# Sliding the right-side tiles of SBUF by 480 bytes in a gated attention and SwiGLU kernel

## The chip, the cores and the metric

The kernel runs on one core of a Trainium2 chip. The metric is the device time in microseconds of one execution, as a median over runs. The core has five engines with instruction queues of their own: TensorE (PE; its weight loads are shown apart as PEld), VectorE (DVE), ScalarE (ACT), GpSimd (POOL) and SyncE (SP), which here only issues transfers. They work on SBUF, the on-chip memory of 128 partitions, and on PSUM, into which TensorE writes its sums. A tile is an area of SBUF that has the same byte address in every partition.

## The reference

```python
def _A_ref(x, wqkv, wo):                       # x: 1 x 2048 x 512, H = 32 heads of 16
    qkv = (x @ wqkv).reshape(B, S, 3, H, Dh)...
    scores = jnp.einsum("bhqd,bhkd->bhqk", q, k) * Dh ** -0.5
    o = jnp.einsum("bhqk,bhkd->bhqd", softmax(scores), v)
    return o.transpose(0, 2, 1, 3).reshape(B, S, D) @ wo

def _B_ref(x, w1, w3, w2):                     # F = 1792
    return (silu(x @ w1) * (x @ w3)) @ w2

g = sigmoid((x * gate_w).sum(-1, keepdims=True))
out = g * _A_ref(x, wqkv, wo) + (1 - g) * _B_ref(x, w1, w3, w2)
```

All inputs and the output are float32.

## The kernel before

The work is one attention layer with 32 heads over 2048 positions, one SwiGLU layer, and a mix of the two. Products that need float32 accuracy are made of three products of rounded halves (type float32r): high by high, high by low, low by high. A matrix thus appears as two tiles, such as xH and xL for x, fh and fl or wh and wl for weights. In a matmul call the second argument is the stationary operand (the weights that LDWEIGHTS puts into the array), the third the moving one, which streams 512 columns past it.

**Where tiles lie.** SBUF is filled by two stacks. From the left come the pools const, xp (xH0 to xL3, 8 KB each), vp (V), qkp (Qt and Kt, two of each) and, later, wk (p0 to p9 of 4 KB and u of 2 KB). From the right end come fw (slots fr, fh1, fl1, fh3, fl3), fk (slots gw, raw, sg, hx, gs), all of 2048 bytes a partition, and p1 (xn, wh, wl, hi, lo and three small ones), which only the first stage uses. `slot(tag)` takes from fw if the tag begins with f, otherwise from fk. When p1 is closed (`ph1.close()`), wk is opened on the left and grows over the room that p1 had. The names in the profile leave buffer numbers out, so fh stands for fh1 and fh3, and xH also for the tiles that later reuse xp's places (w2H, w2L, Oh, Ol).

**First stage.** x is loaded into xn, transposed by TensorE, and rounded into xH and xL. `project_qk` (L181) multiplies the first 128 columns of Q and of K with weights wh and wl from p1; `project_v`, by `three` (L95 to L97), makes V with xH or xL stationary and the halves fh, fl of the weights moving. `bound` and `guard_rows` work out whether the scores are small enough for a softmax without row maxima; the flag is read at the branch of `row_maxima` (L278, `tc.If`), which all engines pass. Ahead of it SP issues the Q and K transfers for the first heads (L254, L261), and `load_weights(chunks[0])` (L314) loads the first weights, which POOL splits (L321, L322).

**Main stage.** TensorE's order is written out by hand as a string, one letter for each piece of work:

```python
one = "QFFF" * 7 + "QPPPP"
two = ["QFFF" * 5 + "QPPQQPP", "QFFF" * 6 + "PPQQPP"]
order = "QQFFF" + one * LONG + "".join(two[...] for i in range(short))   # LONG = 83, short = 44
```

- Q is `score` (L719): for two heads at once, in the array's rows 0 to 63 and 64 to 127, Kt is stationary (50 rows) and Qt moving, into one of two PSUM tiles S. ScalarE turns S into p by exp (L723).
- F is `feed`: up to two matmuls of 64 rows, "upper" and "lower", each with weights of its own, of a product that has nothing to do with attention. In turn these are `w_product` (L409: the other Q and K columns, then w1 and w3; stationary are the halves in fh, fl, raw or gw, moving xH or xL), `h_product` (L518: the SwiGLU's last product; stationary are tiles of fw and fk that hold h by the list SETS, moving the halves of w2 in xp), and `o_product` (L597: part of the output projection; stationary are again tiles of fw and fk).
- P is `pv` (L706): V is stationary (17 columns), p moving, four at once for two units and two heads, into acc. `evac` (L687) copies acc to u after each head pair.

So a long period holds 8 Q, 21 F and 4 P, a short one 8 Q, 15 F and 4 P. VectorE copies out the sums and works on the silu (L432 to L458), POOL splits later weights (L488, L489) and multiplies by reciprocals (L578).

**Last stage.** Two row blocks of the output projection take their weights (ot) from raw and gw; then eight blocks take them from xp and, for the last quarter, from tiles of wk that VectorE has just written (L816). All use `three`, twelve matmuls of 128 rows a block, with wo in xp and wk tiles moving.

Of the kernel before, what the change touches and what calls it, by code (L numbers as in the profile page):

```python
# [8 lines left out]
F32 = mybir.dt.float32  # L9
# [8 lines left out]
P = 128  # L18
# [15 lines left out]
def gated_mix_kernel(ctx: ExitStack, tc: tile.TileContext, x, wqkv, wo, w1, w3, w2, gate_w, out):  # L34
# [25 lines left out]
    xp = ctx.enter_context(tc.tile_pool(name="xp", bufs=1))  # L60
    vp = ctx.enter_context(tc.tile_pool(name="vp", bufs=1))
    qkp = ctx.enter_context(tc.tile_pool(name="qkp", bufs=1))
    fw = ctx.enter_context(tc.tile_pool(name="fw", bufs=2, side="right"))
    fk = ctx.enter_context(tc.tile_pool(name="fk", bufs=2, side="right"))
    ph1 = ExitStack()
# [782 lines left out]
```

## Time and profile before

| | |
|---|---|
| median of 3 runs | 1423.19 us (1422.14 to 1423.74) |
| span of the profiled execution, first to last instruction | 1417.6 us |
| median less that span | 5.6 us |
| TensorE busy | 1408.8 us, 99% |
| ScalarE busy | 1033.2 us, 73% |
| VectorE busy | 449.4 us, 32% |
| GpSimd busy | 321.1 us, 23% |
| HBM traffic | 98 GB/s over the span |

The profile gives one execution. Its times run from the first instruction on. In a view in order of time, a row gives the start and the length in us, the engine, the line, the operation, output<-inputs with the moving operand ahead of the stationary one, and how many instructions are merged (x2). A busy time of TensorE contains overlap: matmuls are pipelined, and the next begins before the last has drained, so the distance of two starts tells more than the length of one. In a view of groups the numbers behind the bar are the busy time in us and the mean length of one in ns; in a view of one line they are the least, median and greatest length in ns. A window row gives the stretch, its length, then the busy time and count of each engine.

### The profile page before, as it was taken

The numbers are of one execution on the slowest core, as the hardware profiler recorded it, in microseconds if no ns is written. First come the engines' busy times: TensorE is split into PE (matmuls) and PEld (weight loads), VectorE is DVE, ScalarE is ACT, GpSimd is POOL, SyncE is SP. The second block draws the span as 40 slices with busy tenths as digits, with TensorE's granted clock in tenths as the row PEclk, the third lists the DMA queues.
The fourth block names the chain that finished last, engine by engine and source line by source line (L and its number), as shares of the span: only waits on it lengthen the run. The fifth ranks groups of instructions, "written<-read, shape, count | busy, mean of one in ns | idle before, by whom it ended". The sixth has DMA issues, their size and how long they took to land.

```text
span 1417.6 us, 28518 instructions
## 1 busy us (share of the span) xinstructions
PE 1408.8 (99%) x11399; PEld 833.7 (59%) x11399; DVE 449.4 (32%) x845; ACT 1033.2 (73%) x1153; POOL 321.1 (23%) x356
## 2 busy tenths in 40 slices
PE   9999999999999999999999999999999999999998
PEld 7865656656556566565565665655555555554556
DVE  4421102464555545455464545400000000000013
ACT  4556767777777777777777777777788778877870
POOL 5014443011011100110110015441332332233230
PEclk9999999999999999999999999999999999999999
DMA  7554455342124432223233234543534443345445
GB/s 197 141 121 114 126 140 128 73 110 69 46 61 85 113 69 61 70 72 87 68 76 79 76 81 122 136 101 74 126 81 102 104 105 70 66 112 106 106 133 182
DMA packets 112668, 141.42 MB, mean 100 GB/s; under 512 B 16400, under 2 KB 70672, under 8 KB 109456
## 3 DMA queue, kind: packets, MB, share of 16 engines
q1 hardware_dynamic: 110384, 135.72, 39.6%
q10 hardware_dynamic: 2144, 3.80, 0.8%
q8 instruction: 92, 1.51, 0.5%
q14 instruction: 48, 0.39, 0.1%
HBM read 90.70 MB, written 48.76 MB: 98 GB/s over the span
## 4 chain that ended last, share of the span: by engine, by line
PE 93%; POOL 0%; DMA 0%; DVE 0%; ACT 0%; issue 0%; SPq 0%; ACTq 0%; POOLq 0%
PE acc L706 32%; PE f L409 27%; PE S L719 19%; PE f L518 11%; PE f L597 1%; PE f L95 0%; PE f L97 0%; PE f L96 0%; DMA fr<-in_B_w_dram 0%; PE S L97 0%; PE S L96 0%; PE S L95 0%; POOL xL L489 0%; POOL fl L489 0%; DVE sg L458 0%; POOL xH L488 0%
## 5 line engine op out<-in xcount | busy, mean ns | idle before, releaser
L723 ACT ACTIVATE p<-S 128x1024 f32<-128x1024 f32 x1024 | 967.5, 1026 | 308.4 <-PE S L719 307.1
L706 PE MATMUL acc<-p,V 128*17 128x512 f32 x4096 | 473.5, 594 | 0.0
L719 PE MATMUL S<-Qt,Kt 50*128 50x512 f32 x2048 | 427.9, 413 | 1.1 <-POOLq L278 0.6
L719 PEld LDWEIGHTS S<-Qt,Kt 50*128 50x128 f32 x2048 | 193.8, 184 | 187.4 <-ACT p L723 80.4
L706 PEld LDWEIGHTS acc<-p,V 128*17 128x17 f32 x4096 | 102.8, 97 | 274.1 <-issue 273.9
L409 PE MATMUL f<-xL,fh 64*128 64x512 f32 x1024 | 205.1, 391 | 0.0
L409 PE MATMUL f<-xH,fl 64*128 64x512 f32 x1024 | 204.9, 390 | 0.0
L409 PE MATMUL f<-xH,fh 64*128 64x512 f32 x1024 | 204.7, 390 | 0.0
L440 DVE RECIPROCAL sg<-sg 128x64 f32<-128x64 f32 x448 | 201.2, 509 | 1.9
L409 PEld LDWEIGHTS f<-xL,fh 64*128 64x128 f32 x1024 | 99.4, 187 | 21.2
L409 PEld LDWEIGHTS f<-xH,fl 64*128 64x128 f32 x1024 | 98.5, 185 | 20.1
L409 PEld LDWEIGHTS f<-xH,fh 64*128 64x128 f32 x1024 | 99.4, 187 | 17.7
L321 POOL CAST fh<-fr 128x512 fp32r<-128x512 f32 x32 | 21.6, 674 | 371.1 <-DMA fr<-in_B_w_dram 246.5
L687 DVE COPY u<-acc 128x512 f32<-128x512 f32 x32 | 22.1, 692 | 257.0 <-PE acc L706 257.0
L518 PE MATMUL f<-xH,fl 64*128 64x512 f32 x224 | 82.2, 391 | 0.5 <-POOL fl L489 0.5
L518 PE MATMUL f<-xL,fh 64*128 64x512 f32 x224 | 82.2, 391 | 0.3 <-POOL xL L489 0.3
L518 PE MATMUL f<-xH,fh 64*128 64x512 f32 x224 | 82.1, 391 | 0.0
L518 PE MATMUL f<-xH,raw 64*128 64x512 f32 x192 | 74.9, 390 | 0.0
L532 DVE TENSOR_SCALAR gs<-f,omg 128x512 f32<-128x512 f32 x16 | 12.0, 751 | 176.4 <-PE f L518 176.4
L432 DVE COPY gs<-f 128x512 f32<-128x512 f32 x56 | 38.7, 691 | 78.1 <-PE f L409 78.1
L518 PE MATMUL f<-xH,fr 64*128 64x512 f32 x160 | 62.4, 390 | 0.0
L454 DVE TENSOR_TENSOR raw<-f,gs 128x512 f32<-128x512 f32 x50 | 34.1, 682 | 82.7 <-PE f L409 82.7
(216 smaller groups left out, 1309.6 us busy)
## 6 DMA issues: line engine op xcount, KB each, us to landing
Kt<-kH_d SPq DMA_DIRECT2D x128, 128.0 KB
h_d<-sg SPq DMA_DIRECT2D x56, 256.0 KB
sg<-h_d SPq DMA_DIRECT2D x43, 256.0 KB
fr<-in_B_w_dram SPq DMA_DIRECT2D x42, 256.0 KB
Qt<-qH_d SPq DMA_DIRECT2D x128, 64.0 KB
Kt<-kL_d SPq DMA_DIRECT2D x64, 128.0 KB
fr<-in_A_wqkv_dram SPq DMA_DIRECT2D x18, 256.0 KB
Qt<-qL_d SPq DMA_DIRECT2D x64, 64.0 KB
```

The lines of the kernel that those rows point to most:

```text
L321: nc.gpsimd.tensor_copy(wh, r)
L409: nc.tensor.matmul(ps, w[i == 2][r, k, :], (xL if i == 1 else xH)[b][r, k, :], start=n == 0 and r.start == 0, stop=n == 3 * ND - 1 and r.s ...
L432: nc.vector.tensor_copy(gs, ps)
L440: small.append(lambda q=q: nc.vector.reciprocal(sg[:, q:q + 64], sg[:, q:q + 64]))
L454: nc.vector.tensor_mul(gu, ps, st["gs"])
L518: nc.tensor.matmul(ps, hs[t][q][i == 2][r, P * o:P * o + P], (w2L if i == 1 else w2H)[q][r, o, :], start=n == 0 and r.start == 0, stop=n = ...
L532: nc.vector.tensor_scalar(y, ps, omg[:, t:t + 1], None, op0=OP.mult)
L597: nc.tensor.matmul(ps, ot[t][i == 2][r, P * k:P * k + P], wo_[k][i == 1][r, :], start=n == 0 and r.start == 0, stop=n == 3 * ND - 1 and r. ...
L687: nc.vector.tensor_copy(u, acc)
L706: nc.tensor.matmul(acc[r:r + DH + 1, :], V[:, k, 2 * j + h, :], p[:, h, :], start=k == 0, stop=k == NT - 1)
L719: nc.tensor.matmul(ps[:, h, :], Kt[i][r:r + 50, P * k:P * k + P], Qt[i][r:r + 50, t:t + 512], start=True, stop=True)
L723: nc.scalar.activation(p, ps, AF.Exp, scale=SCALE)
```

## The change

A pool with one tile of 480 bytes a partition (120 float32) is opened on the right side ahead of all others. Nothing reads or writes it. It is never closed before the end, so every tile of fw, fk and p1 begins 480 bytes lower: at a multiple of 64 bytes, where it was 32 bytes past one. The left pools and every instruction stay as they are.

```diff
     qkp = ctx.enter_context(tc.tile_pool(name="qkp", bufs=1))
+    top_pad = ctx.enter_context(tc.tile_pool(name="top_pad", bufs=1, side="right"))
+    top_pad.tile([P, 120], F32, name="top_pad")
     fw = ctx.enter_context(tc.tile_pool(name="fw", bufs=2, side="right"))
     fk = ctx.enter_context(tc.tile_pool(name="fk", bufs=2, side="right"))
```

## The prediction

> **What bounds the kernel now.** I read the page first, then the order of time on TensorE in one period of the main stage, then the last thirty microseconds, then the chain of waits at the few places where TensorE stops.
>
> ```profile
> span 1417.6 us, 28518 instructions
> PE 1408.8 (99%) x11399; PEld 833.7 (59%) x11399; DVE 449.4 (32%) x845; ACT 1033.2 (73%) x1153; POOL 321.1 (23%) x356
> PEclk9999999999999999999999999999999999999999
> PE 93%; POOL 0%; DMA 0%; DVE 0%; ACT 0%; issue 0%; SPq 0%; ACTq 0%; POOLq 0%
> ```
>
> TensorE works 99% of the span at full clock, and 93% of the chain that ended last is its own work. So a change counts by what it does to the pitch of matmuls, the time from one start to the next. One period shows that pitch. In a name like f<-xH,fh the first operand is the moving one, the second the stationary one (the weights, loaded ahead by LDWEIGHTS).
>
> ```profile
> 256.10 0.40 PE L719 MATMUL S<-Qt,Kt 50*128 50x512 f32 x2
> 256.33 0.39 PE L409 MATMUL f<-xH,fh 64*128 64x512 f32 x2
> 256.56 0.40 PE L409 MATMUL f<-xL,fh 64*128 64x512 f32 x2
> 256.80 0.40 PE L409 MATMUL f<-xH,fl 64*128 64x512 f32 x2
> 257.03 0.40 PE L719 MATMUL S<-Qt,Kt 50*128 50x512 f32 x2
> ...
> 261.67 0.39 PE L719 MATMUL S<-Qt,Kt 50*128 50x512 f32 x2
> ```
>
> Rows of x2 are two 64-row matmuls that share the array. From 256.10 to 261.67 there are six cycles of one score pair and three feed pairs, 24 starts in 5.57 us: 0.928 us a cycle, 232 ns a pair. Nothing here waits; the question is whether 232 ns is the floor. The end of the kernel answers it. There the output projection runs 128-row matmuls of the same 512 columns, first with weights from right-side tiles (raw, gw), then from left-side tiles (xH, xL, p).
>
> ```profile
> 1386.63 0.40 PE L95 MATMUL f<-xH,raw 128*128 128x512 f32 x1
> ...
> 1391.30 0.39 PE L97 MATMUL f<-p,gw 128*128 128x512 f32 x1
> 1391.53 0.39 PE L95 MATMUL S<-xH,xH 128*128 128x512 f32 x1
> ...
> 1412.61 0.39 PE L95 MATMUL S<-p,p 128*128 128x512 f32 x1
> ```
>
> By the code (twelve matmuls a block of 128 rows) 21 start from 1386.63 up to 1391.53: 233.3 ns each. From there to 1412.61 it is 93: 226.7 ns each. The step falls on the first matmul with left-side weights; the moving tiles are the same (xH, xL, p) on both sides of it, and the pitch then holds to the end, whichever PSUM tile is written. The shape view says it too:
>
> ```profile
> L95 PE MATMUL f<-p,raw 128*128 128x512 f32 x4 | 1.6, 394 | 0.0
> L95 PE MATMUL S<-p,xH 128*128 128x512 f32 x4 | 1.6, 389 | 0.0
> L95 PEld LDWEIGHTS f<-p,raw 128*128 128x128 f32 x4 | 0.8, 188 | 0.2
> L95 PEld LDWEIGHTS S<-p,xH 128*128 128x128 f32 x4 | 0.8, 188 | 0.2
> ```
>
> The same moving p is streamed in 394 ns with right-side weights and in 389 ns with left-side ones, while the load itself reads 188 ns in both. So a tax of 233.3 - 226.7 = 6.6, say **6.7 ns a matmul**, sits on weights from the right side. What differs about these tiles is where they begin: the change says 32 bytes past a multiple of 64, while the layout of the left pools (xp, qkp, wk) puts xH, xL, Kt, Qt and p at multiples of 512. The right side can be taxed as a moving operand as well:
>
> ```profile
> L95 PE MATMUL f<-fh,xH x64: 392/396/502, 23.5 to 83.9; 128*128 128x512 f32 x64
> L95 PE MATMUL S<-xH,xH x8: 389/389/389, 1391.5 to 1398.3; 128*128 128x512 f32 x8
> ```
> In the projection of V, fh moves and xH is the weight: never below 392 ns, median 396, against 389 in all eight of the last stage.
>
> **The change part by part.** No instruction is added or removed; every tile of fw, fk and p1 slides down by 480 bytes. All their slots (2048 bytes in fw and fk) and the weight slices (512 bytes) are multiples of 64, so one slide moves all of them from 32 past to 0. The tiles of wk take over p1's room later; worked out from the sizes, each of p0 to p9 and u lies over the same p1 tiles after the slide as before, so no wait is added.
>
> *Feed matmuls.* Their weights are all right-side tiles (fh, fl, raw, gw, fr, hx).
>
> ```profile
> 0.00:1417.60 1417.60, 472.52 (x3264) 315.40 (x3264) 1.00 0.41 100
> 0.00:1417.60 1417.60, 206.84 (x1344) 137.55 (x1344) 1.00 0.41 100
> 0.00:1417.60 1417.60, 27.50 (x144) 18.33 (x144) 1.00 0.41 100
> ```
>
> These are the matmuls of L409, L518 and L597 over the whole span: 3264 + 1344 + 144 = 4752, in pairs 2376. Is the tax a pair's, too? The steady cycle has three taxed pairs and one score pair with left operands: 4 x 226.7 + 3 x 6.7 = 926.9 ns, where 928 was read. The sum fits the pair as it fits the single matmul, so 2376 x 6.7 = **15.9 us** go, all on the path. Bounds: nothing, if the right side itself is what costs, and 2376 x 7.2 = 17.1 us if the whole cycle's excess over 4 x 226.7 (21 ns, three ways 7.1) goes. I take 6.7, the row that compares tiles directly. The 24 late matmuls of the tail give 24 x 6.7 = 0.2 us.
>
> *Early stage.* 192 matmuls with moving fh or fl and 96 with weights wh, wl (L181) carry about 7 ns each, 2.0 us at most. But what opens the main stage is not TensorE:
>
> ```profile
> 63.22 1.09 PE L181 MATMUL S<-xH,wl 128*128 128x512 f32 x4
> 76.31 2.19 SPq L314 DMA_DIRECT2D fr<-in_A_wqkv_dram  x2
> 81.27 0.61 POOL L321 CAST raw<-fr 128x512 fp32r<-128x512 f32 x1 [43.43 <-DMA fr<-in_A_wqkv_dram]
> 83.90 1.28 POOL L322 TENSOR_TENSOR gw<-fr,raw 128x512 fp32r<-128x512 f32 x1
> 85.33 0.93 PE L719 MATMUL S<-Qt,Kt 50*128 50x512 f32 x4 [0.61 <-POOLq L278]
> ```
>
> The branch at L278 waits for POOL's split of the first weights, which waits for a load issued at 76.31, behind SP's row of Q and K transfers that began with the last L181 product. So only what TensorE saves before 64.3 us arrives: nine of 16 V tiles (108 matmuls) and the 96, less those that ran in the first 26 us beside loads. About 140 x 6.7 = **0.9 us**, between 0 and 2.0.
>
> *V as weights* (L706) and p as its stream stay where they are, on the left; a block of 32 keeps its time.
>
> ```profile
> 251.57 3.56 PE acc L706 x32
> ```
>
> *Other users of the moved tiles* are priced by left and right rows of one shape:
>
> ```profile
> L687 DVE COPY u<-acc 128x512 f32<-128x512 f32 x32 | 22.1, 692 | 257.0 <-PE acc L706 257.0
> L432 DVE COPY gs<-f 128x512 f32<-128x512 f32 x56 | 38.7, 691 | 78.1 <-PE f L409 78.1
> L578 POOL TENSOR_TENSOR p<-p 128x512 f32<-128x512 f32 x6 | 7.7, 1288 | 0.0
> L489 POOL TENSOR_TENSOR fl<-sg,fh 128x512 fp32r<-128x512 f32 x23 | 29.6, 1287 | 1.8
> ```
>
> 692 against 691 and 1288 against 1287 ns: zero. Transfers into the moved tiles could go either way; TensorE's work hides them except at the two places shown here (the load above, 81.27 - 76.31 = 5.0 us, and the one below), and I take zero, with 1 us either way (a tenth of the 5.0 us at each). Without that cover, a load's 5 us would count whole.
>
> *Who is late next.* Two things do not shrink with TensorE.
>
> ```profile
> L723 ACT ACTIVATE p<-S 128x1024 f32<-128x1024 f32 x1024 | 967.5, 1026 | 308.4 <-PE S L719 307.1 <-ACT p L723 1.3
> 255.66 6.61 ACT L723 ACTIVATE p<-S 128x1024 f32<-128x1024 f32 x7 [2.97 <-PE S L719]
> 1118.79 1.94 ACT L723 ACTIVATE p<-S 128x1024 f32<-128x1024 f32 x2 [1.25 <-PE S L719]
> 909.52 0.69 DVE hx L454
> ...
> 922.64 0.50 PE f L518
> ```
>
> Two exps back to back take 1.94 us, and one takes 1.026 (its group's mean), so ScalarE's own pitch is 0.92 us. Today a score comes every 0.928; afterwards every 4 x 226.7 = 0.907, so ScalarE falls behind by 14 ns a score for the seven scores up to the block of L706. The slack is there: the exp that began at 255.66 ended near 256.69, and the score that reuses its PSUM tile began at 257.03, 0.34 us later; after the change at worst 0.34 - 2 x 0.02 - 6 x 0.014 = 0.21 remain. Queued behind a blocked score are the three feed pairs and the L706 block, so it would cost TensorE directly; I take 0.3 us in all for places already tight. The other is a chain of 13.1 us from VectorE (909.52) over a load and POOL to TensorE (922.64); TensorE, 1.3% faster there, waits 0.2 us longer. In the tail the last operand is split in time:
>
> ```profile
> 1404.94 0.69 DVE L816 TENSOR_TENSOR p<-fr,p 128x512 fp32r<-128x512 f32 x1 [0.70 <-ACT p L815]
> ```
> It ends at 1405.6. The last 24 matmuls read it; the one at 1412.61 is the 22nd of them, so the first starts at 1412.61 - 21 x 0.2267 = 1407.85, 2.2 us later, far more than the 0.2 us that the tail gains.
>
> **The sum.** 15.9 + 0.2 + 0.9 - 0.3 - 0.2 = 16.5 us off the profiled 1417.6: a span of 1401.1. The median of the runs, 1423.19, is 5.6 above the span; I keep that: **1406.7 us**.
>
> **The rivals.** *ScalarE takes over.* If the slack does not carry, each run of eight scores is paced at 0.921 instead of 0.907: 7 x 14 = 98 of the 141 ns (21 x 6.7) saved per long period come back, and 5 x 14 = 70 of 100 (15 x 6.7) per short one. With 83 long and 44 short periods by the code, 83 x 43 + 44 x 30 = 4.9 us remain, with the early 0.9 some 5.8: 1417.4. For it: 0.92 is above 0.907. Against: 0.34 us of slack, a fresh start after every L706 block.
>
> *The side, not the residue.* If weights from these tiles are slow because they were just written by POOL, or lie high in SBUF, the slide does nothing: 1423. For it: no row has a right-side tile at a multiple of 64. Against: the moving fh is taxed alike, long after it was written; and the last 24 matmuls take their weights p 2.2 us after VectorE wrote them, at 226.7 ns.
> The Trainium skill (SBUF — State Buffer, Specifications) has SBUF cachelines of 16 bytes and a penalty for each crossing to a new one. By that rule 512 contiguous bytes cross equally often from 32 past as from 0, so the change would be worth nothing and this rival's time would hold; the trace's 394 against 389 disagrees unless the side is the cause.
>
> *A collision, slower.* After the slide the tiles of fw and fk begin at multiples of 512 bytes, at the same residue as the stream xH that runs while they load; today they lie 480 past. If two reads at equal places collide, from the first feed pair on, at a price like today's tax on top of it, 2376 x 6.7 = 15.9 come on: 1439. Against: in the tail both operands are at multiples of 512 and run fastest.
>
> **How the numbers follow.** Forecast 70%, ScalarE 13%, no effect 11%, collision 6%. The forecast's own range is 1403 to 1410 (early and transfers 2 us, the tax's bounds 1 us, waits 3 us). The range for 8 in 10 takes in the ScalarE case: 1402.5 to 1418. Within 0.2%, 2.8 us, is what can't be told from no change: faster 0.83, same 0.11, slower 0.06.
>
> **What would show it.** The cycle from 256.10 should read 0.907 instead of 0.928, matmuls of L95 with raw weights 389 instead of 394, fh as moving operand 389. A block of L706 stays at 3.56 us. If scores begin to wait on L723 in every period, ScalarE has taken over; if raw still reads 394, the residue was not the cause, and the prediction is wrong.

## The result and the profile after

The change brings no gain: a median of 1420.63 us over 14 runs (1419.80 to 1426.29), against 1420.56 us (1417.92 to 1423.74) for 14 runs of the kernel before. The ratio is 1.0006, with a 95% interval of 0.9995 to 1.0018. The forecast was 1406.7 us, its range 1402.5 to 1418. In some executions the granted clock halves for some 9 us early in the main stage, which costs about 5 us (last section); those without it, told by their clock or, for the kernel before, by their time, take 1419.80 to 1421.01 us after the change and 1417.92 to 1418.97 before, so that like for like the change costs about 1.5 us.

From the page of the kernel after: the span, the engines, and the groups of the scores and of the feeds (all line numbers are two higher than before).

```profile
span 1417.7 us, 28518 instructions
PE 1409.3 (99%) x11399; PEld 833.6 (59%) x11399; DVE 448.7 (32%) x845; ACT 1035.4 (73%) x1153; POOL 320.5 (23%) x356
L721 PE MATMUL S<-Qt,Kt 50*128 50x512 f32 x2048 | 426.9, 412 | 1.4 <-POOLq L280 0.9
L411 PE MATMUL f<-xH,fh 64*128 64x512 f32 x1024 | 207.3, 396 | 0.0
L411 PE MATMUL f<-xL,fh 64*128 64x512 f32 x1024 | 205.5, 392 | 0.0
L411 PE MATMUL f<-xH,fl 64*128 64x512 f32 x1024 | 204.5, 390 | 0.0
```

The feeds, which were to become 6.7 ns cheaper, read 396, 392 and 390 ns. Before, the same groups read 390, 391 and 390:

```profile
L409 PE MATMUL f<-xL,fh 64*128 64x512 f32 x1024 | 205.1, 391 | 0.0
L409 PE MATMUL f<-xH,fl 64*128 64x512 f32 x1024 | 204.9, 390 | 0.0
L409 PE MATMUL f<-xH,fh 64*128 64x512 f32 x1024 | 204.7, 390 | 0.0
```

Only the feed that comes right behind a score has changed, and for the worse. The kernel after in order of time on TensorE, at five places:

```profile
83.64 0.93 PE L721 MATMUL S<-Qt,Kt 50*128 50x512 f32 x4 [0.87 <-POOLq L280]
...
253.86 0.50 PE L721 MATMUL S<-Qt,Kt 50*128 50x512 f32 x2
...
255.83 0.40 PE L721 MATMUL S<-Qt,Kt 50*128 50x512 f32 x2
256.06 0.40 PE L411 MATMUL f<-xH,fh 64*128 64x512 f32 x2
256.30 0.40 PE L411 MATMUL f<-xL,fh 64*128 64x512 f32 x2
256.53 0.39 PE L411 MATMUL f<-xH,fl 64*128 64x512 f32 x2
...
260.49 0.39 PE L721 MATMUL S<-Qt,Kt 50*128 50x512 f32 x2
...
264.37 0.50 PE L721 MATMUL S<-Qt,Kt 50*128 50x512 f32 x2
...
1386.06 0.50 PE L97 MATMUL f<-xH,raw 128*128 128x512 f32 x1
1386.39 0.40 PE L98 MATMUL f<-xL,raw 128*128 128x512 f32 x1
...
1388.93 0.39 PE L97 MATMUL f<-xH,raw 128*128 128x512 f32 x1
...
1391.65 0.39 PE L97 MATMUL S<-xH,xH 128*128 128x512 f32 x1
```

- The first score starts at 83.64 instead of 85.33. Other profiles with the same first stage scatter: 84.60, 85.11 and 85.36 without the pad (runs of the experiments below), 83.90 and 84.45 with it. The means, 85.10 and 84.00, are 1.1 us apart.
- Five cycles of one score and three feeds take 260.49 - 255.83 = 4.66 us, 0.932 a cycle, where 0.928 was read before. A long period (first score behind a block of L708 to the next such score) is 264.37 - 253.86 = 10.51 us. Its median over the main stage went from 10.495 to 10.518, that of a short period from 9.427 to 9.433.
- From the first score to the first matmul of the last stage it is now 1386.06 - 83.64 = 1302.4 us; before it was 1385.83 - 85.33 = 1300.5. So the main stage lost 1.9 us and gave the early gain back; the medians of the periods say the same, 83 x 0.023 + 44 x 0.006 = 2.2 us.
- In the last stage, the second block with weights from raw and gw (twelve matmuls, 1388.93 to 1391.65) runs at 226.7 ns, as predicted, where it ran at 233.3. The block ahead of it does not yet: 11 starts from 1386.39 to 1388.93 are 231 ns apart.

So the tail shows the effect, the main stage does not. In V's projection it shows as well, in the first products of Q and K only in part: their medians go from 397 to 393 or 394 ns, not to 389 (rows of two lines of the kernel after, least, median and greatest length in ns):

```profile
L97 PE MATMUL f<-fh,xH x64: 388/389/496, 22.9 to 81.9; 128*128 128x512 f32 x64
L183 PE MATMUL S<-xH,wl x32: 387/394/496, 11.3 to 62.4; 128*128 128x512 f32 x32
```

### The profile page after: what moved, and what is told of

Same layout as the page of the kernel before. It is cut to its first block, busy times and chain, and to the rows that moved or that the text cites. A ratio compares the mean times of both kernels' runs of the same rounds, so it can differ in the third digit from the quotient of the medians.

```text
span 1417.7 us, 28518 instructions
## 1 busy us (share of the span) xinstructions
PE 1409.3 (99%) x11399; PEld 833.6 (59%) x11399; DVE 448.7 (32%) x845; ACT 1035.4 (73%) x1153; POOL 320.5 (23%) x356
## 4 chain that ended last, share of the span: by engine, by line
PE 92%; POOL 1%; DMA 1%; SPq 0%; issue 0%; ACT 0%; DVE 0%; ACTq 0%; POOLq 0%
PE acc L708 32%; PE f L411 27%; PE S L721 19%; PE f L520 11%; PE f L599 1%; DMA fr<-in_B_w_dram 1%; POOL xL L491 0%; PE f L97 0%; PE f L98 0%; PE f L99 0%; SPq L256 0%; PE S L98 0%; PE S L97 0%; PE S L99 0%; POOL xH L490 0%
## 5 line engine op out<-in xcount | busy, mean ns | idle before, releaser
L725 ACT ACTIVATE p<-S 128x1024 f32<-128x1024 f32 x1024 | 969.9, 1027 | 308.0 <-PE S L721 306.7
L708 PE MATMUL acc<-p,V 128*17 128x512 f32 x4096 | 473.5, 594 | 0.0
L721 PE MATMUL S<-Qt,Kt 50*128 50x512 f32 x2048 | 426.9, 412 | 1.4 <-POOLq L280 0.9
L721 PEld LDWEIGHTS S<-Qt,Kt 50*128 50x128 f32 x2048 | 194.4, 184 | 187.9 <-ACT p L725 79.8
L708 PEld LDWEIGHTS acc<-p,V 128*17 128x17 f32 x4096 | 102.7, 97 | 273.4 <-issue 273.2
L411 PE MATMUL f<-xH,fh 64*128 64x512 f32 x1024 | 207.3, 396 | 0.0
L520 PE MATMUL f<-xH,fh 64*128 64x512 f32 x224 | 83.0, 395 | 0.0
```

What stands on the lines that cost most here:

```text
L411: nc.tensor.matmul(ps, w[i == 2][r, k, :], (xL if i == 1 else xH)[b][r, k, :], start=n == 0 and r.start == 0, stop=n == 3 * ND - 1 and r.s ...
L520: nc.tensor.matmul(ps, hs[t][q][i == 2][r, P * o:P * o + P], (w2L if i == 1 else w2H)[q][r, o, :], start=n == 0 and r.start == 0, stop=n = ...
L708: nc.tensor.matmul(acc[r:r + DH + 1, :], V[:, k, 2 * j + h, :], p[:, h, :], start=k == 0, stop=k == NT - 1)
L721: nc.tensor.matmul(ps[:, h, :], Kt[i][r:r + 50, P * k:P * k + P], Qt[i][r:r + 50, t:t + 512], start=True, stop=True)
L725: nc.scalar.activation(p, ps, AF.Exp, scale=SCALE)
```

## The experiments

Each run below is called after its question. Most of these kernels were run once. Their times stand beside a time of the kernel before that was taken with them; the argument rests on pitches, not on these times.

**Three other sizes of the pad: is it the place modulo 64 that counts?** By the layout, weights in fw and fk lie 224 past a multiple of 256 bytes before the change and at 0 after; xH and xL, which stream past them (and are the weights in V's projection, where fh streams), are at 0 throughout. The tiles wh and wl of p1 lie at 96 before and at 128 after. Pads of 32, 224 and 352 bytes in place of the 480 put fw and fk at 192, 0 and 128, and p1 at 64, 128 and 0. The first of them reads:

```diff
-    top_pad.tile([P, 120], F32, name="top_pad")
+    top_pad.tile([P, 8], F32, name="top_pad")
```

> 480 is replaced by 32 bytes: right-side tiles of fw and fk begin at multiples of 64 bytes too, but 448 past a multiple of 512. Theory A (the residue of 64 counts for full 128-row matmuls only; pairs of 64 rows have a floor of their own): a long period stays at 10.47 to 10.53 us, the projection of V keeps 226.7 ns a matmul once it has run ten or so. Theory B (weights and stream at the same residue of 512 collide in the main stage, which ate the gain): a long period drops to about 10.35 us and the span to about 1402.

> 480 is replaced by 224 bytes: the tiles of fw and fk begin 256 past a multiple of 512, as far as can be from the stream's residue. A: a long period 10.47 to 10.53 us. B: 10.35 us or less, the best of all pads.

> 480 is replaced by 352 bytes: the tiles of fw and fk begin 128 past a multiple of 512, those of p1 at a multiple of 256. A: a long period 10.47 to 10.53 us, and L183 (weights of p1) as with 480 bytes. B: between e1 and e2, about 10.35 us.

Measured: 1425.18, 1420.85 and 1426.94 us, beside 1423.05 before. Long periods have medians of 10.516, 10.519 and 10.573 us: no place brings the main stage under the 10.495 of before. At 128 past a multiple of 256 it is slower than at the others, 0.05 us a long period; why stays open. Rows of V's projection, one from each pad in that order, the last with a row of the Q and K products:

```profile
L97 PE MATMUL f<-fh,xH x64: 392/394/498, 22.9 to 83.5; 128*128 128x512 f32 x64
```

```profile
L97 PE MATMUL f<-fh,xH x64: 388/389/497, 23.6 to 82.5; 128*128 128x512 f32 x64
```

```profile
L97 PE MATMUL f<-fh,xH x64: 390/394/501, 23.2 to 83.2; 128*128 128x512 f32 x64
L183 PE MATMUL S<-xH,wl x32: 388/389/496, 11.6 to 63.3; 128*128 128x512 f32 x32
```

fh is at a multiple of 64 in all three, yet reads 389 ns only where it lies at a multiple of 256, like its partner xH. And wl, slow after the change, reads 389 with the 352-byte pad, which puts just it at a multiple of 256. So in an unbroken series of 128-row matmuls the fast pitch came with weights and stream both at multiples of 256 bytes, whichever side the tile is on. A place modulo 64 is not enough, and theory A, which had V's projection at 226.7 ns with the 32-byte pad, was wrong there. Whether the two must lie at multiples of 256 or only at the same place modulo 256 stays open, since no run has both at one other place. Nor is it all or nothing: in the last stage the weights at 192 past (32-byte pad) run at 229 ns a matmul (21 steps from 1392.13 to 1396.94), between 227 and 233. The collision of two operands at equal places, the prediction's slower rival, falls: with both at multiples of 256 they are the fastest.

**Pairs in the quiet tail: do pairs of 64 rows have a floor of their own at 232 ns?** From the kernel before, eight blocks of the last stage are run as pairs of 64-row matmuls, all operands on the left at multiples of 512, with next to nothing for ScalarE to do (1.27 us busy of the 17 from 1390).

```diff
-    for t in range(NT // 2, NT):
-        for n in range(ND - 1):
-            project(t, n)
+    for t in range(NT // 2, NT, 2):
+        for flip in range(2):
+            for n in range(ND - 1):
+                two = zip(halves(t + flip, n, slice(0, 64)), halves(t + 1 - flip, n, slice(64, P)))
...
+                    nc.tensor.matmul(banks[t], us, um, start=first, stop=False)
+                    nc.tensor.matmul(banks[t + 1], ls, lm, start=first, stop=False)
```

> The kernel before, but in the last stage the blocks 8 to 15 run their first nine products of each as pairs of 64 rows, upper rows of the one block beside lower rows of the next, all operands left-side tiles at multiples of 512; each block's sum gets other rows than it should, the number of starts is the same. Theory A (a pair has a floor of its own): the pairs start every 231 to 234 ns, as in the main stage. Rival A2 (pairs are as good as full matmuls; it is the change of kind between score and feed that costs): they start every 226.7 ns, as the full ones did.

Measured: 1418.89 us beside 1423.05. The upper halves (L819) in order of time:

```profile
1391.95 0.39 PE L819 MATMUL S<-p,xH 64*128 64x512 f32 x1
...
1392.63 0.39 PE L819 MATMUL S<-xH,xH 64*128 64x512 f32 x1
1392.86 0.39 PE L819 MATMUL S<-xL,xH 64*128 64x512 f32 x1
```

Four steps in 0.91 us: a pair runs at 227 ns. There is no floor at 232 for pairs, so something in the main stage keeps them from it.

**Thin exps: is it ScalarE?** In the kernel after, eight of the ten exps of L725 work on 16 of the 512 columns of each half.

```diff
+        if n < 8 and n in kept:
+            p = kept[n]
+            nc.scalar.activation(p[:, :, 0:16], ps[:, :, 0:16], AF.Exp, scale=SCALE)
+        else:
             p = wk.tile([P, 2, 512], F32, name=f"p{n}")
             nc.scalar.activation(p, ps, AF.Exp, scale=SCALE)
```

> The changed kernel (480 bytes), but eight of ten exps (those into p0 to p7, after the first into each) work on 16 of 512 columns a head, so p holds old values there; ScalarE is nearly idle in those score periods and busy in the two of ten that go into p8 and p9. Theory C (ScalarE's exp, reading PSUM and writing SBUF beside TensorE, keeps the feed matmuls from the 226.7 ns pace): the cycles of one score and three feeds without a full exp take 0.907 us, those beside a full one 0.933. Theory D (the alternation of score and feed alone does it): all cycles stay at 0.933 us.

Measured: 1418.05 us beside 1422.78. The exps now take 198 ns, and five cycles of TensorE still take 4.67 us, 0.934 each; the long period's median is 10.514:

```profile
255.12 0.40 PE L723 MATMUL S<-Qt,Kt 50*128 50x512 f32 x2
...
259.79 0.40 PE L723 MATMUL S<-Qt,Kt 50*128 50x512 f32 x2
```

ScalarE is not the bound. What is left to try is TensorE's own order of work.

**Scores among the pairs: does the mix do it?** To the pairs of the tail a score pair of 50 rows is added ahead of every three, its sums going into the same banks.

```diff
+                for h in range(2):
+                    r = slice(64 * h, 64 * h + 50)
+                    nc.tensor.matmul(banks[t + h], Kt[1][r, c:c + P], Qt[1][r, 0:512], start=first, stop=False)
```

> The kernel before with the last stage as in e4, pairs of 64 rows of left-side tiles, but ahead of every three pairs one score pair (Kt, Qt, 50 rows) is added into the same sums, so the stage has 24 more starts and the output changes; ScalarE is idle there. C: after some ten starts the pace is 226.7 ns for all, 0.907 us a cycle. D: a cycle of one score and three pairs takes 0.93 us, as in the main stage.

Measured: 1429.95 us beside 1422.78. In order of time:

```profile
1396.72 0.40 PE L821 MATMUL S<-Qt,Kt 50*128 50x512 f32 x2
1396.95 0.40 PE L823 MATMUL S<-xH,xH 64*128 64x512 f32 x1
...
1397.19 0.39 PE L823 MATMUL S<-xL,xH 64*128 64x512 f32 x1
...
1398.58 0.40 PE L821 MATMUL S<-Qt,Kt 50*128 50x512 f32 x2
```

Two cycles in 1.86 us, 0.93 each, with steps of 233, 237, 233 and 231 ns: the main stage's pattern, with ScalarE and GpSimd idle from 1396 to 1400 and with every operand at a multiple of 256. Transfers are dense there (a DMA share of 1.03), but as dense (1.00) in the tail with 50 rows throughout below, which is fast. Taking the scores in costs the pairs their 227.

**Longer runs of feeds.** If a score throws TensorE out of its pace, six feeds in a row should find it again. Ten long periods of the kernel after get the order below.

```diff
+    runs = ["QQFFFFFF" * 3 + "QFFFQPPPP"]
```

> The changed kernel, but in ten of the 83 long periods the order is two scores, then six feeds, where it was one and three. C: ScalarE is as busy as before, so the six feeds run at 232 to 238 ns each on the mean, as they do now. D: with half the alternations the last of the six feeds come down to 227 ns.

Measured: 1439.49 us beside 1422.78; the ten periods take 10.98 us each, since the second score of each two may wait for an exp (the first row), which makes this no remedy. They are 4.6 us of the loss. The rest lies mostly in the first period, where the clock fell to 0.50, and in the last stage, where TensorE waits 4.09 us for VectorE (L604) behind transfers. The upper and lower halves have drifted apart by some 20 ns; below, behind the wait of a second score, stand two matmuls of one half that are three starts apart:

```profile
420.40 0.50 PE L721 MATMUL S<-Qt,Kt 50*128 50x512 f32 x2 [0.23 <-ACT p L725]
...
423.07 0.39 PE L411 MATMUL f<-xH,fl 64*128 64x512 f32 x1
...
423.75 0.39 PE L411 MATMUL f<-xH,fl 64*128 64x512 f32 x1
```

Three starts in 0.68 us, 227 ns each. In each of the ten periods the last two or three steps of a run of six come down to 226 or 227 ns, though not in all runs of six. So these feeds, with these weights, can run at the fast pitch beside everything else that the main stage does.

**The same number of rows: in the tail and in the main stage.** What tells a score from a feed is 50 rows against 64. In the tail, the pairs are cut to 50 rows as well (the tail's mix above, with `slice(0, 50)` and `slice(64, 114)`). In the main stage, scores are made over 64 rows, where the added 14 rows of Qt are filled with zeros once; that goes on top of the change, and, as its counterpart, on the kernel before.

```diff
+    def fill_q():
+        zero = slot("sg", F32)
+        nc.gpsimd.memset(zero, 0.0)
...
+                    nc.gpsimd.tensor_copy(Qt[i][r:r + 32, 512 * j:512 * j + 512], zero[r:r + 32, :])
...
-            nc.tensor.matmul(ps[:, h, :], Kt[i][r:r + 50, P * k:P * k + P],
-                             Qt[i][r:r + 50, t:t + 512], start=True, stop=True)
+            nc.tensor.matmul(ps[:, h, :], Kt[i][r:r + 64, P * k:P * k + P],
+                             Qt[i][r:r + 64, t:t + 512], start=True, stop=True)
```

> The kernel of e6 with the pairs, too, over 50 rows of each half (their sums lack 14 rows of 64), so that score and pairs have one number of rows. E: after some ten starts all run at 226.7 ns, 0.907 us a cycle. F: 0.933 us a cycle as in e6.

> The changed kernel (480 bytes), with the score matmuls over 64 rows instead of 50: rows 50 to 63 and 114 to 127 of Qt are set to zero once in the first stage, so the sums are the same. Theory E (a change of the number of rows between score and feed throws TensorE out of its 226.7 ns pace): the main stage settles at 226.7 ns, a long period goes from 10.52 to about 10.35 us, a short one from 9.43 to about 9.33, and the span falls by some 18 us to 1400. Theory F (another property of the score, such as its tiles or its PSUM tile, does it): a long period stays at 10.52 us and the time at 1420.

> The kernel before (no pad, the tiles of fw and fk 224 past a multiple of 256) with the same 64-row scores. If both the rows and the residue are needed for the 226.7 ns pace: a long period stays near 10.49 us and the time near 1420. If rows alone do it: 10.35 us.

The tail with 50 rows throughout (1428.69 us beside a median of 1418.93) runs four cycles in 3.62 us, 0.905 each, all at 227 ns:

```profile
1396.83 0.39 PE L821 MATMUL S<-Qt,Kt 50*128 50x512 f32 x2
...
1400.45 0.39 PE L821 MATMUL S<-Qt,Kt 50*128 50x512 f32 x2
```

So 50 rows are as fast as 64 while nothing changes from one matmul to the next. The main stage with 64-row scores and the pad:

```profile
span 1404.4 us, 28529 instructions
```

```profile
252.56 0.51 PE L730 MATMUL S<-Qt,Kt 64*128 64x512 f32 x2
...
256.36 0.39 PE L730 MATMUL S<-Qt,Kt 64*128 64x512 f32 x2
...
259.08 0.39 PE L730 MATMUL S<-Qt,Kt 64*128 64x512 f32 x2
...
262.96 0.50 PE L730 MATMUL S<-Qt,Kt 64*128 64x512 f32 x2
```

```profile
L420 PE MATMUL f<-xH,fl 64*128 64x512 f32 x1024 | 205.8, 388 | 0.0
L420 PE MATMUL f<-xH,fh 64*128 64x512 f32 x1024 | 205.6, 388 | 0.0
L420 PE MATMUL f<-xL,fh 64*128 64x512 f32 x1024 | 205.6, 388 | 0.0
```

Three cycles in 2.72 us: 0.907 each, the number that the prediction asked for. The period is 262.96 - 252.56 = 10.40 us (median 10.393; short 9.340). The time is **1406.55 us** (1406.06 to 1406.84, 4 runs) against 1418.93 (13 runs); the ratio is 0.9902, with an interval of 0.9877 to 0.9927. This beats both kernels. The gain is less than the 18 us that were expected, mostly since each block of L717 (L708 before) starts the series anew: on the mean over the long periods the first steps behind it read 233, 233, 232, 230, 229 and 229 ns. The same rows without the pad:

```profile
256.01 0.39 PE L728 MATMUL S<-Qt,Kt 64*128 64x512 f32 x2
...
261.57 0.39 PE L728 MATMUL S<-Qt,Kt 64*128 64x512 f32 x2
```

Six cycles in 5.56 us, 0.927 each, and 1420.05 us (1417.26 to 1422.56, 10 runs), a ratio of 0.9997 (0.9980 to 1.0014): nothing beyond the 0.015 us a long period in the table. Of the four combinations only one is fast:

| scores over | weights of feeds modulo 256 | span, us | cycle, us | long period, median us |
|---|---|---|---|---|
| 50 rows | 224 (before) | 1417.6 | 0.928 | 10.495 |
| 50 rows | 0 (after) | 1417.7 | 0.932 | 10.518 |
| 64 rows | 224 | 1416.1 | 0.927 | 10.480 |
| 64 rows | 0 | 1404.4 | 0.907 | 10.393 |

## Why the prediction was wrong

**The step that failed** is the one that carried the tail's 6.7 ns into the main stage: "The sum fits the pair as it fits the single matmul, so 2376 x 6.7 = 15.9 us go, all on the path." The 6.7 ns are real, but they are not a tax that each matmul pays for its own weights. In these runs TensorE finds the pitch of 226.7 ns only in a series in which weights and stream lie at multiples of 256 bytes and the number of rows stays the same; a break of the series can throw it back to a mean near 232 for up to nine starts. The tail before the change broke only the first condition, the main stage broke both, so mending the first gave nothing there. That 4 x 226.7 + 3 x 6.7 came to 926.9 beside the 928 read was a coincidence, and the working used it as the proof. The prediction had no row of a pair at the fast pitch with a score beside it; the tail's rows were all of one shape, 128 rows, while the main stage alternates 50 and 64. By the starts above, the term measured a loss of 1.9 us where a gain of 15.9 was forecast. With both conditions met the main stage takes 1288.7 us from its first score to the last stage (84.09 to 1372.78), 11.8 less than the 1300.5 of before.

**The bound of that term** was too narrow too. "Nothing, if the right side itself is what costs" was the only way to zero that the prediction saw, at 11%. The answer was that side, residue and size all were right in the tail and the term was still nil. (The upper bound had a slip: 21 ns over three pairs is 7.1 a pair, 16.9 us, not 7.2 and 17.1.)

**The early stage** was about right: 1.1 us between the means (1.7 in the two main profiles), 0.9 forecast within 0 to 2.0. V's products reach 389 ns. The products with wh and wl gave about 3 ns of the 8, since the slide put them at 128 past a multiple of 256; so the size has some luck in it.

**The tail**: 0.1 us measured (5.59 us from the first raw matmul to the first left-side one, 5.70 before), 0.2 forecast. The first block pays for the start of a series.

**Waits**: one score alone waits for ScalarE, 0.5 us (L721's idle time is 1.4 us in all, as listed above), so the rival that ScalarE takes over had no occasion. With the fast version's 0.907 cycle it had one, and that cycle held, but not by the slack. From 1.94 and 1.026 us ScalarE's pitch comes to 0.914, not 0.92, and in the fast version exps follow each other in 0.907:

```profile
258.68 1.04 ACT L734 ACTIVATE p<-S 128x1024 f32<-128x1024 f32 x1
```

```profile
259.59 1.05 ACT L734 ACTIVATE p<-S 128x1024 f32<-128x1024 f32 x1
```

The second begins 0.51 us behind its score (259.08, shown above), as the one before it did. ScalarE does not fall behind by 14 ns a score, and the slack was not drawn on.

**No effect, for another reason.** The rival that gave 1423 assumed that the side costs, not the place. Its time came nearest, but its ground fell: the same right-side tiles read 394 or 389 ns by their place alone. The Trainium skill (SBUF — State Buffer, Specifications) has cachelines of 16 bytes with a penalty for each crossing, and by that rule the 32-byte pad and the 480-byte pad would read alike; the runs' 394 against 389 disagrees.

**From span to median**: "5.6 above the span; I keep that" was wrong by 3.6. One execution lies 2 us above its own span (1418.38 with a span of 1416.5). The three runs shown at first, 1422.14 to 1423.74, have times like those with the halved clock (last section); the profile is of an execution at full clock.

## What to carry to other kernels

A difference of pitch seen in one stage is a term for another stage only if the other stage runs the same series: same rows, same mix, no breaks; look for a row of the stage itself at the better pitch before multiplying. Where TensorE is the bound, try weights and stream at multiples of 256 bytes and pad neighbouring matmuls to one number of rows, and do both, since here each alone was worth next to nothing and the two together 12 us of 1419. When a sum of two small terms fits a reading, ask what else gives the same sum.

## What the runs showed of the hardware that was not expected

**The pace of a series.** In the kernel after, the starts of the first 128-row matmuls of the last stage (from 1386.39) lie 235, 233, 236, 224, 231, 236, 228, 233, 231 ns apart, then 226 to 227 without end. With the 224-byte pad the row is the same within 1 ns. In the fast version it is shorter, 231, 236, 228, 233, 231, and in the kernel before the step from right-side to left-side weights (1391.53) goes to 227 at once. So the number of starts that a break costs varies here from none to nine. Why 256 bytes, and why a change of rows counts, stays open: no run looks inside TensorE's reading of SBUF. The Trainium skill (TensorE: Matmul & The Clock Gate, Part 1) gives 215.7 ns from start to start for 512 columns at full clock; no series of these kernels comes below 226.

**A clock that halves early in some executions.** Windows over the first main period in the run with the 32-byte pad (stretch, length, TensorE's busy time and count, granted clock, share of DMA, GB/s), and the same of the kernel after:

```profile
84.00:90.00 6.00, 4.71 (x19) 0.75 0.36 105
90.00:95.00 5.00, 5.00 (x17) 0.50 0.91 121
95.00:100.00 5.00, 5.00 (x37) 0.78 0.02 3
```

```profile
90.00:95.00 5.00, 5.00 (x45) 1.00 0.67 85
```

The granted clock is 0.50 over the whole middle stretch, and 17 matmul records stand there instead of 45. It costs about 5 us: the kernel before takes near 1418.5 us with a mean clock of 1.000 and near 1423.3 with 0.996.
